# Soft-MoE after a gated recurrence: two output rows of batch 3 from the last weight's chunks, a slot sum in two PSUM banks

## The chip, the cores and the metric

The kernel runs on one core of one Trainium2 chip. Times are device microseconds of one execution, and lower is better. Engines are named as in the profile: PE is the matmul engine, PEld its weight loads, DVE the vector engine, ACT the scalar engine, POOL the GpSimd engine, SP the engine that issues most DMAs. L12 is line 12 of the kernel that the sentence speaks of; where the two kernels' lines differ, it is said which is meant.

## What is computed

The input is `x` and `f_logit` (4 batches, 5056 tokens, 256 channels). A gated recurrence along the tokens is followed by a soft mixture of 8 experts with 4 slots each (32 slots), weights `w1` (8, 256, 1024) and `w2` (8, 1024, 256):

```python
f = lower_bound + (1 - lower_bound) * sigmoid(f_logit)
h[t] = f[t] * h[t-1] + (1 - f[t]) * x[t]
logits = h @ phi                              # (20224, 32)
d = softmax(logits over all tokens)           # one column per slot
slot_input = d.T @ h                          # (32, 256), four slots per expert
slot_out = relu(slot_input @ w1[e]) @ w2[e]   # (32, 256)
out = softmax(logits over the slots) @ slot_out   # (20224, 256)
```

The output, 20.7 MB in float32, can't begin before the last `w2` has been used, since every token mixes all 32 slots.

## The kernel before

The order of the work is written out by hand (`tc.manual_schedule()`), engine by engine in program order. There are three stages.

**The recurrence** (until about 129 us) streams groups of 512 tokens of each batch: load, sigmoid on ACT, product on POOL, transposes on PE, scan on DVE, logits, exponentials into `etall` (partition 32b+s holds slot s of batch b, all tokens along the free side), and the sum `slot_ps`. The 16 weights are loaded from POOL's queue by `load_w` near its end; the last one, `w2_sb[7]`, comes in three parts of four, two and two chunks (a chunk, index `fc`, is 128 of the 1024 hidden units).

**The slot stage** (129 to 143 us) is a chain. `slot_sb` (L597) is turned by four matmuls into `sin_ps` (L601), which lies in the tile `tail`; DVE and ACT make `sin` of it (L611, L612). 32 matmuls (L628) give `hi_ps`, ACT and DVE the two `hi` tiles (L633, L635). They are transposed (L643) and copied: experts 0 to 3 into `hid` (L652), experts 4 to 7 into `wide` by four copies that ACT and DVE take in turn (L659), each of which waits for the one before. `cs_ps` (L645) and `rcs` (L653) are the softmax sum over tokens and its reciprocal. 32 matmuls (L664) sum experts 0 to 3, then a loop over `j` (L674) adds experts 4 to 7, eight matmuls each, into one PSUM tile `so_ps`; for `j == 0` the sum of the first four experts is added by a float32 matmul (L680). Between them stand the `row_sums` matmuls (L391), which sum the exponentials over the slots: 39 rows of 128 tokens, eight of them ahead of L601, eight after `j == 0`, 23 after `j == 1`; DVE's reciprocals (L683, L687, L688) make `rrow` of them. The calls of `spin` (L152) are matmuls whose result nobody reads. DVE writes `slot_out` (L692), POOL a form of it for pairs of batches, `slot_bd` (L694).

**The output stage** multiplies `etall` by `slot_out`. `whole` (L711, then DVE L701 or ACT L705, then the DMA L735) does a block of 16 rows of 128 tokens for one batch; `couple` (L748, then DVE L756 or ACT L753, DMA L765 or L768) does a block for two batches at once. The first block is that of batch 0, and its first DMA takes rows 0 and 1 (row r of a partition's 16 consecutive tokens): 256 KB. All DMAs of this stage stand in SP's queue in program order.

Of the kernel before, what the change touches and what calls it, by code (L numbers as in the profile page):

```python
# [9 lines left out]
F32 = mybir.dt.float32  # L10
BF16 = mybir.dt.bfloat16
# [7 lines left out]
def kernel(  # L19
# [45 lines left out]


    consts = ctx.enter_context(tc.tile_pool(name="consts", bufs=1))
    ident_f = consts.tile([P, P], F32, name="ident_f")
    make_identity(nc, ident_f)
    ident = consts.tile([P, P], BF16, name="ident")  # L70

    rep = consts.tile([P, B, NS], F32, name="rep")

    lb_row = consts.tile([1, D], F32, name="lb_row")
    nc.scalar.dma_start(out=lb_row, in_=lower_bound.unsqueeze(0))
    lbs = consts.tile([P, 2, DC], F32, name="lbs")
    omlb, nomlb = lbs[:, 0], lbs[:, 1]
    phi_f = consts.tile([P, DC, NS], F32, name="phi_f")
    nc.gpsimd.dma_start(out=phi_f, in_=moe_phi.rearrange("(p o) s -> p o s", o=DC))
    phi = consts.tile([P, DC, NS], BF16, name="phi")  # L80

    nc.vector.tensor_copy(ident, ident_f)

    def rep_constants(b):
# [15 lines left out]
    nc.vector.memset(parity, 0.0)  # L100
    for b in range(B):
        nc.vector.memset(parity[ds(b * NS, NS), ds(b % 2, 1)], 1.0)

    def lb_constants():
        row = lb_row.rearrange("u (p o) -> u p o", o=DC)
# [56 lines left out]
    with tc.tile_pool(name="sp2", bufs=3) as sp2, \  # L162
# [437 lines left out]
        for o in range(DC):  # L600
            nc.tensor.matmul(sin_ps[:, o], slot_v[:, o], rep[:, 0],  # L601
                             start=True, stop=True, skip_group_check=True)

    with tc.tile_pool(name="ew", bufs=1) as ew, \
         tc.tile_pool(name="pm", bufs=2, space=PSUM) as pm, \
         tc.tile_pool(name="pbig", bufs=1, space=PSUM) as pbig:

        rep2 = rep.rearrange("p b s -> p (b s)")

        sin = [ew.tile([P, NS], BF16, name=f"sin{o}") for o in range(DC)]  # L610
        nc.vector.tensor_scalar_mul(sin[0], sin_ps[:, 0], omlb[:, ds(0, 1)])  # L611
        nc.scalar.activation(sin[1], sin_ps[:, 1], ACT.Copy, scale=omlb[:, ds(1, 1)])  # L612

        cs1 = ew.tile([P, 1], F32, name="cs1")
        nc.vector.tensor_reduce(cs1, csum, AX.X, ALU.add)


        Q = 4
        H = F // 2
        his = []  # L620
        for q in range(E // Q):
            hi = ew.tile([P, F], BF16, name=f"hi{q}")
            for k in range(2):
# [12 lines left out]
            his.append(hi)  # L636
        cs_ps = pm.tile([P, 1], F32, name="cs_ps", tag="pm")
        rcs = ew.tile([P, 1], F32, name="rcs")
        for q in range(E // Q):
            ht_ps = psu.tile([P, FC, P], BF16, name="ht_ps", tag="up")  # L640
            hi_v = his[q].rearrange("p (c f) -> p f c", f=FC)
            for fc in range(FC):
                nc.tensor.transpose(ht_ps[:, fc], hi_v[:, fc], ident)  # L643
            if q == 0:
                nc.tensor.matmul(cs_ps, rep2, cs1, start=True, stop=True)  # L645
                src = ht_ps.rearrange("p f (j s) -> p f j s", s=NS)[:, :, :, ds(0, SPE)]
                src = bass.AP(tensor=src.tensor, offset=src.offset,
                              ap=[list(src.ap[0]), [P, FC], [NS + SPE, Q], [1, SPE]])
                dst = hid[:, :, :, ds(0, SPE)]
                dst = bass.AP(tensor=dst.tensor, offset=dst.offset,  # L650
                              ap=[list(dst.ap[0]), [Q * NS, FC], [NS + SPE, Q], [1, SPE]])
                nc.scalar.copy(dst, src)  # L652
                nc.vector.reciprocal(rcs, cs_ps)  # L653
                continue
            for j in range(Q):
                s0 = (Q + j) * SPE
                src = ht_ps[:, :, ds(j * NS + s0, SPE)]
                copy = nc.scalar.copy if j % 2 == 0 else nc.vector.tensor_copy
                copy(wide[:, :, j, :, ds(s0, SPE)],  # L659
                     src.unsqueeze(2).broadcast_to([P, FC, B, SPE]))  # L660
        so4_ps = pm.tile([P, D], F32, name="so4_ps", tag="pm")
        for e in range(Q):
            for fc in range(FC):
                nc.tensor.matmul(so4_ps[ds(fc % 4 * NS, NS), :], hid[:, fc, e],  # L664
                                 w2_sb[e][:, fc],
                                 start=(e == 0 and fc < 4),
                                 stop=(e == Q - 1 and fc >= FC - 4),
                                 skip_group_check=True)
        so4 = ew.tile([P, D], F32, name="so4")
        nc.vector.tensor_copy(so4, so4_ps)  # L670
        so_ps = pm.tile([P, D], F32, name="so_ps", tag="pm")
        for j in range(Q):
            for fc in range(FC):
                nc.tensor.matmul(so_ps, wide[:, fc, j].rearrange("p b s -> p (b s)"),  # L674
                                 w2_sb[Q + j][:, fc], start=j == 0 and fc == 0,
                                 stop=j == Q - 1 and fc == FC - 1, skip_group_check=True)
# [12 lines left out]
            if j == 2:  # L689
                spin(tail[:, 0], 6, NS)  # L690
        spin(tail[:, 0], 4, D)
        nc.vector.tensor_scalar_mul(slot_out, so_ps, rcs)  # L692
        for u in range(2):
            nc.gpsimd.tensor_scalar_mul(slot_bd[:, u], slot_out, parity[:, ds(u, 1)])  # L694


    held.close()
    with tc.tile_pool(name="osb", bufs=3) as osb:

        def by_vector(ob, op, scale):  # L700
            nc.vector.tensor_tensor(ob, op, scale.broadcast_to(list(ob.shape)), ALU.mult)  # L701
# [19 lines left out]
        pout = ctx.enter_context(tc.tile_pool(name="pout", bufs=8, space=PSUM))  # L721

        def whole(i, b, pieces, ends):
            n_r = blocks[i][1]
            dst = rows_of(i, b)
            ob = osb.tile([P, n_r, D], F32, name="ob", tag="ob")
            done = 0
            for j, r, k in pieces:
                op = pout.tile([P, 2, D], F32, name="op", tag="op")
                share(op, i, b, r, k)  # L730
                (by_vector, by_scalar)[j](ob[:, ds(r, k)], op[:, ds(0, k)],
                                          scale_of(i, b, r, k))
                if r + k in ends:
                    q = ds(done, r + k - done)
                    nc.sync.dma_start(out=dst[:, q], in_=ob[:, q])  # L735
                    done = r + k
# [35 lines left out]
        def rest():  # L772
# [21 lines left out]
        whole(0, 1, [(t % 2, 2 * t, 2) for t in range(wide_r // 2)], (wide_r,))  # L794
        rest()
        for i in range(end):
            for j in range(B // 2):
                if i or j:
                    couple(i, j)


# [28 lines left out]
```

## Time and profile before

| | us |
|---|---|
| median of the 3 runs (lowest, highest) | 197.96 (197.47, 198.5) |
| the profiled execution's own time | 197.27 |
| its span, first to last instruction | 195.5 |
| PE, DVE, ACT, POOL busy | 152.8, 147.2, 137.3, 103.3 |
| DMA, mean over the span | 362 GB/s |

The page's second part cuts the span into 40 slices of 4.9 us. Its DMA line shows the share of time in which the 16 DMA engines were busy, its PEclk line the clock that was granted to PE, in tenths. PEclk is low in slices 6 and 7 (5 and 8) and in the last ten (5).

### The profile page before, as it was taken

Reading aid. Unit: us, or ns where it says so; the run is one execution under the profiler, and the core shown is the slowest. Engines: PE = TensorE matmul, PEld = TensorE weight load, DVE = VectorE, ACT = ScalarE, POOL = GpSimd, SP = SyncE. Lnnn points to the kernel's source line nnn. Section 1 sums busy time; section 2 is a strip of 40 time slices with the busy share of each in tenths; the row PEclk is TensorE's granted clock in tenths of the full one; section 3 lists DMA queues with packets and bytes.
Section 4 is the critical chain, followed back from the end, with each engine's and each line's share of the span. In section 5 each row is a group of like instructions: output and inputs, shape, how many; then the busy total and the mean of one; then the engine's idle time right before and its main releaser. Section 6 shows DMA issues by size and latency. Waiting matters only on the chain.

```text
span 195.5 us, 3260 instructions
## 1 busy us (share of the span) xinstructions
PE 152.8 (78%) x1205; PEld 105.0 (54%) x1205; DVE 147.2 (75%) x188; ACT 137.3 (70%) x188; POOL 103.3 (53%) x78
## 2 busy tenths in 40 slices
PE   1687589977998979899797887989999999990000
PEld 1465448765685767668586675557974433220000
DVE  2669858999889999999999999814279897771000
ACT  3688674899998998989987597544069987682000
POOL 2589578575999779774969969392030000000000
PEclk9999958999999999999999999999995555555555
DMA  6999999999999999999999999999939999999995
GB/s 206 421 417 424 429 424 429 429 422 393 341 424 431 416 322 427 427 408 347 366 423 413 260 213 214 215 215 213 164 148 420 427 454 419 436 432 429 429 429 221
DMA packets 14145, 70.75 MB, mean 362 GB/s; under 512 B 1569, under 2 KB 2594, under 8 KB 10162
## 3 DMA queue, kind: packets, MB, share of 16 engines
q1 hardware_dynamic: 11504, 62.13, 76.8%
q0 software_dynamic: 2624, 8.42, 21.6%
q8 instruction: 9, 0.15, 0.3%
q14 instruction: 6, 0.05, 0.1%
q10 hardware_dynamic: 2, 0.00, 0.0%
HBM read 58.23 MB, written 20.71 MB: 404 GB/s over the span
## 4 chain that ended last, share of the span: by engine, by line
PE 37%; DVE 26%; ACT 11%; DMA 8%; issue 5%; POOL 2%; SPq 0%; ACTq 0%; DVEq 0%; POOLq 0%
DVE h L313 20%; PE op L748 10%; DMA f_t<-in_f_logit_dram 8%; DVE ht L343 5%; PE hp L326 4%; ACT oc L753 4%; PE sp L261 3%; ACT s_t L235 3%; PE up L267 3%; PE lg L357 2%; POOL u_t L246 2%; PE op L711 2%; PE slot_ps L183 2%; PE so_ps L674 2%; PE slot_ps L408 1%
## 5 line engine op out<-in xcount | busy, mean ns | idle before, releaser
L246 POOL TENSOR_TENSOR u_t<-s_t,x_t 128x1024 bf16<-128x1024 bf16 (+1 forms) x39 | 82.5, 2132 | 23.6 <-ACT s_t L235 10.4
L313 DVE TENSOR_TENSOR_SCAN h<-a,h,up 128x512 bf16<-128x512 f32 (+1 forms) x72 | 87.0, 1252 | 3.5 <-PE up L267 1.8
L235 ACT ACTIVATE s_t<-f_t 128x2048 bf16<-128x2048 f32 (+2 forms) x23 | 38.3, 1668 | 4.0 <-DMA f_t<-in_f_logit_dram 3.7
L326 PE MATMUL hp<-ident_f,h 128*128 128x128 f32 (+1 forms) x160 | 29.4, 308 | 7.9 <-DVE ht L343 6.8
L326 PEld LDWEIGHTS hp<-ident_f,h 128*128 128x128 f32 (+1 forms) x160 | 23.6, 207 | 18.1 <-DVE ht L343 12.4
L748 PE MATMUL op<-slot_bd,etall 64*128 64x512 bf16 x62 | 26.4, 581 | 1.0 <-ACT oc L753 0.3
L295 ACT ACTIVATE a<-sp,lbs 128x1024 f32<-128x1024 bf16 x24 | 25.4, 1112 | 1.3 <-PE sp L261 1.0
L261 PE MATMUL sp<-ident_f,s_t 128*128 128x128 f32 x144 | 21.0, 288 | 6.7 <-ACT s_t L235 4.2
L753 ACT ACTIVATE oc<-op,rrow 128x256 f32<-128x256 f32 x54 | 22.2, 489 | 5.0 <-PE op L748 4.8
L756 DVE TENSOR_TENSOR oc<-op,rrow 128x512 f32<-128x512 f32 x35 | 22.4, 685 | 3.4 <-PE op L748 3.3
L261 PEld LDWEIGHTS sp<-ident_f,s_t 128*128 128x128 f32 x144 | 16.9, 148 | 8.8 <-ACT s_t L235 5.1
L302 ACT ACTIVATE a<-sp,lbs 128x512 f32<-128x512 bf16 (+2 forms) x22 | 17.8, 857 | 3.8 <-PE sp L261 3.5
L267 PE MATMUL up<-ident_f,u_t 64*128 64x64 f32 x192 | 17.6, 229 | 2.1 <-POOL u_t L246 2.1
L183 PE MATMUL slot_ps<-rep,ident_f 128*128 128x256 f32 x54 | 18.2, 432 | 0.6 <-POOL rep L86 0.6
L748 PEld LDWEIGHTS <-etall 64*128 64x128 bf16 x62 | 8.9, 150 | 17.4 <-issue 13.1
L343 ACT COPY ht<-hp 128x512 f32<-128x512 f32 (+1 forms) x18 | 10.5, 583 | 10.2 <-PE hp L326 10.2
L267 PEld LDWEIGHTS up<-ident_f,u_t 64*128 64x128 f32 x192 | 13.9, 138 | 6.0 <-POOL u_t L246 2.5
L343 DVE COPY ht<-hp 128x512 f32<-128x512 f32 (+1 forms) x22 | 14.7, 668 | 2.4 <-PE hp L326 2.4
L705 ACT ACTIVATE ob<-op,rrow 128x256 f32<-128x256 f32 x15 | 6.0, 475 | 7.7 <-PE op L711 7.7
L313 DVE TENSOR_TENSOR_SCAN h<-a,up 128x512 bf16<-128x512 f32 x8 | 9.3, 1208 | 2.5 <-ACT a L302 1.7
L183 PEld LDWEIGHTS slot_ps<-rep,ident_f 128*128 128x128 f32 x54 | 8.8, 199 | 3.0 <-issue 1.1
L261 PE MATMUL up<-ident_f,u_t 128*128 128x128 f32 x48 | 9.5, 329 | 0.7 <-POOL u_t L246 0.6
(110 smaller groups left out, 148.3 us busy)
## 6 DMA issues: line engine op xcount, KB each, us to landing
f_t<-in_f_logit_dram SPq DMA_DIRECT2D x12, 1024.0 KB, 11.7
x_t<-in_x_dram SPq DMA_DIRECT2D x12, 1024.0 KB, 11.1
out_dram<-oc SPq DMA_DIRECT2D x6, 2048.0 KB, 13.1
w_sb<-in_moe_w_dram POOLq DMA_DIRECT2D x14, 512.0 KB, 9.7
f_t<-in_f_logit_dram SPq DMA_DIRECT2D x12, 512.0 KB, 8.5
x_t<-in_x_dram SPq DMA_DIRECT2D x12, 512.0 KB, 8.6
out_dram<-ob SPq DMA_DIRECT2D x1, 2048.0 KB, 10.4
out_dram<-oc SPq DMA_DIRECT2D x2, 896.0 KB, 6.9
```

What stands on the lines that cost most here:

```text
L183: nc.tensor.matmul(slot_bank[:, 1], ident_f, wide_rep, start=False, stop=False, skip_group_check=True)
L235: nc.scalar.activation(s_t, f_t, ACT.Sigmoid, scale=-1.0)
L246: nc.gpsimd.tensor_tensor(uts[n][:, :r], s_t[:, :r], x_t[:, :r], ALU.mult)
L261: nc.tensor.transpose(ps[:, :, r], t[:, r], ident_f)
L267: nc.tensor.transpose(v[:, :, r], t(r)[k].bitcast(F32), ident_f[k, k])
L295: nc.scalar.activation(a, sp[:, :, :, :, o], ACT.Identity, scale=nomlb[:, ds(o, 1)], bias=1.0)
L313: nc.vector.tensor_tensor_scan(h[:, :T, o], decays[n // 2, o][:, n % 2, :T], up[:, :T, o], hs[number(g - 1, b)][:, ds(used(g - 1) - 1, 1), ...
L326: nc.tensor.transpose(hp[:n_p, r], hw[:, :n_p, r], ident_f)
L343: copy(hts[g][:n_p, b].rearrange("p r d -> p (r d)").bitcast(F32), hps.pop(n)[:n_p].rearrange("p r c -> p (r c)"))
L748: nc.tensor.matmul(op.rearrange("p u d -> p (u d)"), ew[:, :, r], slot_bd[ds(j * 2 * NS, 2 * NS)].rearrange("s u d -> s (u d)"), start=Tru ...
L753: nc.scalar.activation(ob[:, u, r], op[:, u], ACT.Copy, scale=scale[:, r, ds(u, 1)])
L756: nc.vector.tensor_tensor(ob[:, :, r], op, scale[:, r].unsqueeze(2).broadcast_to([P, 2, D]), ALU.mult)
```

## The change

All lines here are those of the changed kernel. Four things change.

- **Constants share a tile.** `ident_f`, `ident`, `rep` and `lb_row` become views of one tile `base`; its space is used again for the two rows `begun`. A new column `own` (a reduction on DVE at the start, L104) is 1 on the partitions of the last expert's slots.
- **Two rows of batch 3 directly.** The last expert's hidden values times `own * rcs` are written as `hm` by POOL (L671, 32 partitions by 512 elements, after a product of one column on DVE, L669). Four matmuls (L686) multiply them with the exponentials of two rows, and DVE and ACT copy the two results (128 by 512 each) to `gain` (L688). `add` (L698) then multiplies `gain` by the last four chunks of `w2_sb[7]`, straight into the two rows' PSUM sums. What the other experts and chunks give comes by `slot_pre` (L706, L729). ACT and DVE scale the two rows (L738, L740), and SP sends them as the first output DMA (L742, 256 KB). The block that `whole` does first is batch 3's, from row 2 on, with DMAs of 2, 2, 4 and 6 rows; its second call does batch 2, and the pairs of batches that remain are chosen to match.
- **The slot sum in two banks.** `so_ps` ends after the first four chunks of the last weight and is scaled to `slot_so` (L705); a second tile takes the last four chunks, and `slot_out` is made of both (L732).
- **Order and waits.** 11 row sums move from the loop to just behind the `sin_ps` matmuls (L605), five to before the transposes (L640); 4 stay at `j == 0`, 11 at `j == 1`. Of the spins, the two groups of five and the group of four go, and the group of six becomes eight. The pools of the output stage get `reuse_waits="tile"`: an instruction waits for the earlier users of its own tile's space, not for those of the whole pool's.

In the program as built, PE's order from the last expert sums on is: the 32 matmuls L677; the four L686, the first of which waits for POOL's `hm`; `j == 0`, the float32 matmul (L717, waits for DVE's `so4`, which stands behind the copy to `gain` in DVE's queue), four row sums; `j == 1`, 11 row sums and the left-over rows; `j == 2`, eight spins, which wait for DVE's reciprocals; then `j == 3` as in the diff. DVE's `sin` (L614) waits for the last of the 11 row sums that now follow `sin_ps`, since both are in the tile `tail`; in the kernel before, it waits for the last `sin_ps` matmul. DVE's product L669 stands behind its second copy to `wide` (L663).

```diff
+    own = lbs[:, 2, ds(0, 1)]
+    nc.vector.tensor_reduce(own, ident_f[:, ds(P - SPE, SPE)], AX.X, ALU.add)
...
             nc.tensor.matmul(sin_ps[:, o], slot_v[:, o], rep[:, 0],
                              start=True, stop=True, skip_group_check=True)
+        row_sums(8, 19)
...
             his.append(hi)
+        row_sums(19, 24)
...
+        top = ds((B - 1) * NS, NS)
+        early = etall[top, ds(0, P * wide_r)].rearrange("s (p r) -> s r p", r=wide_r)
+        DIR = 2
+        half = FC // 2
+        nc.vector.tensor_tensor(own, own, rcs, ALU.mult)
+        hm = ew.tile([P, half, P], BF16, name="hm")
+        nc.gpsimd.tensor_scalar_mul(hm[top], his[-1].rearrange("p (c f) -> p f c", f=FC)[
+            top, ds(half, half)], own[top])
+        gain = ew.tile([P, half, DIR, P], BF16, name="gain")
...
+        for i in range(0, half, 2):
+            g_ps = (psu.tile([P, 2, DIR, P], F32, name="g_ps", tag="up") if i == 0 else
+                    pbig.tile([P, 2, DIR, P], F32, name="g_ps", tag="hi_ps0"))
+            for k in range(2):
+                nc.tensor.matmul(g_ps[:, k], hm[top, i + k], early[:, ds(0, DIR)],
+                                 start=True, stop=True, skip_group_check=True)
+            (nc.scalar.copy if i else nc.vector.tensor_copy)(gain[:, ds(i, 2)], g_ps)
...
+        def add(r, fcs, start):
+            for fc in fcs:
+                nc.tensor.matmul(rows_ps[r], gain[:, fc - half, r], w2_sb[E - 1][:, fc],
+                                 start=start and fc == fcs[0], stop=fc == FC - 1,
+                                 skip_group_check=True)
+
         for j in range(Q):
             for fc in range(FC):
+                if j == Q - 1 and fc == half:
+                    nc.vector.tensor_scalar_mul(slot_so, so_ps, rcs)
+                    nc.vector.tensor_copy(slot_pre[top], slot_so[top])
+                    so_ps = pm.tile([P, D], F32, name="so_ps", tag="pm")
...
-                if j == Q - 1 and fc in (FC // 2 - 1, FC // 4 * 3 - 1):
-                    spin(tail[:, 0], 5, NS)
+                if j == Q - 1 and fc == half + 1:
+                    for r in range(DIR):
+                        add(r, (half, half + 1), True)
...
-                row_sums(8, wide_r)
+                row_sums(24, 28)
...
-                row_sums(wide_r, n_grp * R)
+                row_sums(28, n_grp * R)
...
-                spin(tail[:, 0], 6, NS)
-        spin(tail[:, 0], 4, D)
-        nc.vector.tensor_scalar_mul(slot_out, so_ps, rcs)
+                spin(tail[:, 0], 8, NS)
+        for r in range(DIR):
+            nc.tensor.matmul(rows_ps[r], early[:, r], slot_pre[top],
+                             start=False, stop=False, skip_group_check=True)
+            add(r, (FC - 2, FC - 1), False)
+        nc.vector.scalar_tensor_tensor(slot_out, so_ps, rcs, slot_so, ALU.mult, ALU.add)
...
+        for r in range(DIR):
+            scale = rrow[:, r, ds(B - 1, 1)]
+            if r == 0:
+                nc.scalar.activation(begun[:, r], rows_ps[r], ACT.Copy, scale=scale)
+            else:
+                nc.vector.tensor_tensor(begun[:, r], rows_ps[r], scale.broadcast_to([P, D]),
+                                        ALU.mult)
+        nc.sync.dma_start(
+            out=out[ds((B - 1) * S, P * wide_r)].rearrange(
+                "(p r) d -> p r d", r=wide_r)[:, ds(0, DIR)], in_=begun)
...
-    with tc.tile_pool(name="osb", bufs=3) as osb:
+    with tc.tile_pool(name="osb", bufs=3, reuse_waits="tile") as osb:
...
-        whole(0, 0, ((0, 0, 1), (1, 1, 1), (0, 2, 2), (1, 4, 2), (0, 6, 2), (1, 8, 2),
-                     (0, 10, 2), (1, 12, 2), (0, 14, 2)), (2, 4, 8, 12, 16))
+        whole(0, B - 1, ((0, 2, 1), (1, 3, 1), (0, 4, 2), (1, 6, 2), (0, 8, 2),
+                         (1, 10, 2), (0, 12, 2), (1, 14, 2)), (4, 6, 10, 16))
```

More of the change, by code (lines that the diff above doesn't have):

```diff
@@ L67 @@
     consts = ctx.enter_context(tc.tile_pool(name="consts", bufs=1))
-    ident_f = consts.tile([P, P], F32, name="ident_f")
+    phi_f = consts.tile([P, DC, NS], F32, name="phi_f")
+    phi = consts.tile([P, DC, NS], BF16, name="phi")
+    base = consts.tile([P, 2 * P + P // 2 + D], F32, name="base")
+    ident_f = base[:, ds(0, P)]
     make_identity(nc, ident_f)
-    ident = consts.tile([P, P], BF16, name="ident")
-    rep = consts.tile([P, B, NS], F32, name="rep")
-    lb_row = consts.tile([1, D], F32, name="lb_row")
+    ident = base[:, ds(P, P // 2)].bitcast(BF16)
+    rep = base[:, ds(P + P // 2, P)].rearrange("p (b s) -> p b s", b=B)
+    lb_row = base[ds(0, 1), ds(2 * P + P // 2, D)]
+    begun = base[:, ds(0, 2 * D)].rearrange("p (r d) -> p r d", r=2)
     nc.scalar.dma_start(out=lb_row, in_=lower_bound.unsqueeze(0))
-    lbs = consts.tile([P, 2, DC], F32, name="lbs")
+    lbs = consts.tile([P, 4, DC], F32, name="lbs")
     omlb, nomlb = lbs[:, 0], lbs[:, 1]
-    phi_f = consts.tile([P, DC, NS], F32, name="phi_f")
+    own = lbs[:, 2, ds(0, 1)]
     nc.gpsimd.dma_start(out=phi_f, in_=moe_phi.rearrange("(p o) s -> p o s", o=DC))
-    phi = consts.tile([P, DC, NS], BF16, name="phi")
     nc.vector.tensor_copy(ident, ident_f)
@@ L671 @@
         so_ps = pm.tile([P, D], F32, name="so_ps", tag="pm")
+        slot_so = ew.tile([P, D], F32, name="slot_so")
+        slot_pre = ew.tile([P, D], BF16, name="slot_pre")
+        rows_ps = [tail[:, 0, ds(0, D)], psu.tile([P, 2, D], F32, name="row_ps", tag="up")[:, 0]]
+        def add(r, fcs, start):
[3 more added lines that the diff above has]
+                                 skip_group_check=True)
         for j in range(Q):
             for fc in range(FC):
+                if j == Q - 1 and fc == half:
+                    nc.vector.tensor_scalar_mul(slot_so, so_ps, rcs)
+                    nc.vector.tensor_copy(slot_pre[top], slot_so[top])
+                    so_ps = pm.tile([P, D], F32, name="so_ps", tag="pm")
                 nc.tensor.matmul(so_ps, wide[:, fc, j].rearrange("p b s -> p (b s)"),
-                                 w2_sb[Q + j][:, fc], start=j == 0 and fc == 0,
-                                 stop=j == Q - 1 and fc == FC - 1, skip_group_check=True)
-                if j == Q - 1 and fc in (FC // 2 - 1, FC // 4 * 3 - 1):
-                    spin(tail[:, 0], 5, NS)
+                                 w2_sb[Q + j][:, fc],
+                                 start=(j, fc) in ((0, 0), (Q - 1, half)),
+                                 stop=j == Q - 1 and fc in (half - 1, FC - 1),
+                                 skip_group_check=True)
+                if j == Q - 1 and fc == half + 1:
+                    for r in range(DIR):
+                        add(r, (half, half + 1), True)
             if j == 0:
@@ L719, in rows_of @@
             return out[ds(b * S + t0, P * n_r)].rearrange("(p r) d -> p r d", r=n_r)
-        pout = ctx.enter_context(tc.tile_pool(name="pout", bufs=8, space=PSUM))
+        pout = ctx.enter_context(tc.tile_pool(name="pout", bufs=8, space=PSUM, reuse_waits="tile"))
         def whole(i, b, pieces, ends):
@@ L726, in whole @@
             ob = osb.tile([P, n_r, D], F32, name="ob", tag="ob")
-            done = 0
+            done = pieces[0][1]
             for j, r, k in pieces:
@@ L789 @@
         end = len(blocks) - 1
-        whole(0, 0, ((0, 0, 1), (1, 1, 1), (0, 2, 2), (1, 4, 2), (0, 6, 2), (1, 8, 2),
-                     (0, 10, 2), (1, 12, 2), (0, 14, 2)), (2, 4, 8, 12, 16))
+        whole(0, B - 1, ((0, 2, 1), (1, 3, 1), (0, 4, 2), (1, 6, 2), (0, 8, 2),
+                         (1, 10, 2), (0, 12, 2), (1, 14, 2)), (4, 6, 10, 16))
         couple(end, 0, (4, 7))
         couple(end, 1)
-        whole(0, 1, [(t % 2, 2 * t, 2) for t in range(wide_r // 2)], (wide_r,))
+        whole(0, B - 2, [(t % 2, 2 * t, 2) for t in range(wide_r // 2)], (wide_r,))
         rest()
@@ L797 @@
             for j in range(B // 2):
-                if i or j:
+                if i or j < B // 2 - 1:
                     couple(i, j)
```

## The prediction

> **What bounds the kernel now.** I read the slices first, then the busy times by stage, then the slot stage instruction by instruction. The page's slices:
>
> ```profile
> PEclk9999958999999999999999999999995555555555
> DMA  6999999999999999999999999999939999999995
> GB/s 206 421 417 424 429 424 429 429 422 393 341 424 431 416 322 427 427 408 347 366 423 413 260 213 214 215 215 213 164 148 420 427 454 419 436 432 429 429 429 221
> ```
>
> From slice 31 on the DMA engines are full to the end: the output stage runs at the rate of its writes. Slice 30 is the only one with a hole. The windows around it (us, busy time of five engines, PE clock, DMA share, GB/s):
>
> ```profile
> 140.00:141.00 1.00, 1.00 (x13) 0.79 (x11) 0.76 (x2) 0.00 (x0) 0.00 (x0) 1.00 0.78 128
> 141.00:142.00 1.00, 1.00 (x22) 0.93 (x21) 0.00 (x0) 0.00 (x0) 0.00 (x0) 1.00 0.23 37
> 144.00:145.00 1.00, 0.98 (x9) 0.83 (x8) 1.00 (x3) 1.00 (x4) 0.97 (x2) 1.00 0.08 25
> 145.00:146.00 1.00, 0.97 (x5) 0.65 (x6) 1.00 (x3) 1.00 (x4) 0.00 (x0) 1.00 1.05 404
> ```
>
> The weights are in by 142, the first output moves just before 145, then the writes never stop until 193.4. So the end is the issue of the first output DMA plus a constant, and I price the change by that one instant. The timeline of the chain up to it (start, length):
>
> ```profile
> 135.91 0.22 DVE L659 COPY wide<-ht_ps 128x128 bf16<-128x128 bf16 x1 [0.33 <-ACT wide L659]
> ...
> 142.06 0.38 PE L674 MATMUL so_ps<-w_t,wide 128*128 128x256 bf16 x2
> ...
> 142.47 0.48 DVE L692 TENSOR_SCALAR slot_out<-so_ps,rcs 128x256 bf16<-128x256 f32 x1 [1.54 <-PE so_ps L674]
> ...
> 144.09 3.10 SPq L735 DMA_DIRECT2D out_dram<-ob  x5
> ```
>
> The last weight part is issued at 127.5 and lands 14.6 us later (the shortest of the four in the view of tile `w_t`), at 142.06: the last two L674 start on it. PE is no less tight: of 135.80 to 142.06 its windows show no idle time, and only the 16 short spins (0.025 us each) are free there. From 142.06 to the issue at 144.09 it takes 2.03 us.
>
> **The change, step by step.** Lines of the changed kernel; times on the clock of this profile.
>
> *Row sums moved forward.* 23 of them took 1.54 us at 138.59, so 0.06 each. DVE's `sin` now waits for 11 of them: 0.66 later. Five more stand before the transposes, 0.3, of which about 0.2 falls where PE waited for `hi` (L628's last start to L643). I take 0.7 for the whole chain from `sin` on, so the last copy to `wide` ends at 136.13 + 0.7 = 136.83, and PE is done with the 32 matmuls of L677 at 135.85 + 0.7 = 136.55. In total PE does no more row sums than before.
>
> *`hm` on POOL.* Behind that copy DVE multiplies a column (0.15, as L653 and L688: 0.17 and 0.11): 136.97. POOL starts 0.19 after its releaser (142.95 to 143.14 at L694): 137.15. The product itself isn't in the trace. Its neighbours:
>
> ```profile
> L694 POOL TENSOR_SCALAR slot_bd<-slot_out,parity 128x256 bf16<-128x256 bf16 x2 | 1.8, 923 | 9.6 <-DVE slot_out L692 9.6
> L115 POOL TENSOR_SCALAR phi<-phi_f,lbs 128x32 bf16<-128x32 f32 x2 | 1.5, 777 | 3.6 <-DMA phi_f<-in_moe_phi_dram 3.6
> L86 POOL COPY rep<-ident_f 32x128 f32<-32x128 f32 x4 | 1.1, 285 | 0.2
> L401 POOL COPY left<-etall 32x64 bf16<-32x64 bf16 x4 | 1.0, 258 | 0.1
> ```
>
> L694 is the same operation with the same factor column: 0.92 for 256 elements. L115's shorter instance takes 0.357 for 32. The line through both gives 512 elements 1.57. Lower end, by the copies on 32 partitions (0.258 for 64, 0.285 for 128): 0.45. Upper end, twice L694: 1.85. I take 1.57, from the nearest row. PE can start L686 at 137.15 + 1.57 + 0.06 = **138.78**, having stood since 136.55: a stall of 2.2 us. Behind L686 in PE's queue is everything that makes `slot_out`.
>
> [...]
>
> *From L686 on PE* (+ counts from its first start): four matmuls of 256 columns, 0.11 each as in L674, +0.44. `j == 0`, eight, +1.31. DVE copies the first pair to `gain` (+0.46, 0.69 as L635) and only then `so4` (0.41, as L670), ready at +1.48, so L717 waits until +1.54. L717 0.44, four row sums 0.25, eight matmuls 0.87, 11 row sums and the left-over 0.72, eight matmuls 0.87: +4.69. The spins wait for the reciprocals (left-over start to spin start was 139.97 to 140.99, so 1.02): +4.78, then 0.2. Four chunks 0.43, two 0.22, four `add` 0.44: the last two chunks start at +6.07, which is 144.85. They landed at 142.06: the wait for the weights is gone, PE is late in its place. `slot_so` (0.48, as L692) and `slot_pre` (0.3, from L82's 0.226 for 128 elements) end at +6.42; the six row matmuls then run to +7.30. DVE makes `slot_out` meanwhile (0.5), then scales row 1 (+7.33, 0.425 as the first L701); SP issues at +7.82 = **146.60**, against 144.09: 2.51 later.
>
> *Edits at no cost.* The reduction at the start (0.15) falls into the 2.6 us in which DVE waits for the first load at L242. Shared constants add no wait in the built order. Tile-wise waits: L701 started 0.42 after L711, a matmul takes 0.27 of it, so at most 0.1 is to be had; I count nothing. SP gets one more DMA ahead of the pairs of batches; its issues are 0.6 apart (five in 3.10), as long as 256 KB take at 404 GB/s, so it keeps up, and the pairs are ready some 4.0 us after the first issue as before (148.13), with 2 MB (4.9 us) in front of them. Bytes and the last DMA are unchanged.
>
> **Sum.** 197.27 + 2.51 = 199.78 on the profiled execution. That one lies 0.69 under the median of 197.96, so 200.5 as a median. With POOL at its ends: 199.4 and 200.8.
>
> **The rivals.**
>
> 1. *PE's clock halves after the stall.* The trace has one idle time of PE as long, and what came of it (timeline, start and length; then the windows, with the clock third from the end):
>
> ```profile
> 23.21 1.09 PE L261 MATMUL sp<-ident_f,s_t 128*128 128x128 f32 x8 [1.96 <-ACT s_t L235]
> ```
>
> ```profile
> 21.00:24.40 3.40, 1.44 (x14) 1.25 (x13) 3.05 (x3) 2.22 (x3) 1.21 (x2) 0.99 1.04 435
> 24.40:27.80 3.40, 2.75 (x16) 1.10 (x13) 2.45 (x2) 3.40 (x3) 3.26 (x3) 0.50 1.01 422
> 27.80:31.20 3.40, 3.40 (x17) 2.95 (x14) 1.84 (x2) 0.46 (x1) 1.87 (x2) 0.50 1.00 424
> 31.20:34.60 3.40, 3.40 (x31) 3.18 (x29) 3.07 (x4) 2.79 (x4) 2.62 (x2) 1.00 1.01 429
> ```
>
> 1.96 us idle, and the clock was half for the next 6.8 us. 16 L711 took 1.97 us at the full clock and 3.63 at half, so a half clock over the 5 us of PE work behind the stall costs up to 3.5, over 3.4 us of it 1.6; I take 2.0: median 202.5. Against it: that window was busy for 1.44 us of 3.4, ours for about 1.6 if it falls alike, and idle times near 1 us changed nothing. [...]
>
> 2. *POOL is quick.* At the copies' rate the stall is 1.1 us: 197.27 + 1.39 = 198.66, median 199.4.
>
> 3. *The change does what it says: faster.* If L686 starts by 135.9, the last chunks are met at 142.06, the six row matmuls end at 143.09, DVE at 143.55, SP issues at 143.62: 0.47 earlier, median 197.5. The point that decides is that start, and PE itself is free only at 136.55; it would need the weights to land some 2.8 us later than here, so that PE's lateness hides.
>
> 4. *Nothing measurable*: the two offset each other, 197.0 to 198.9.
>
> **How the numbers follow.** Forecast 200.5: 0.45. Clock halved, 202.5: 0.26. POOL quick, 199.4: 0.14. Faster, 197.5: 0.08. Within 0.5% (about what a measurement of this kernel tells from no change): 0.07. So slower 0.85, same 0.07, faster 0.08. The range runs from 198.6 to 202.8: it leaves out the faster case, most of "same", and the dearest part of the halved clock, together under 2 in 10. The forecast's own range is 199.6 to 201.0.
>
> **What would show it.** In the profile after: PE L686 waits for POOL's `hm` L671 by 1 us or more; `hm` takes near 1.6; `sin` L614 starts about 0.7 later; the last pair of L708 starts near 144.9, long after the landing; L742 is issued near 146.6; the hole in the DMA grows from 3 to over 5 us. PEclk at 5 between 140 and 147 is rival 1. Wrong if L686 never waits, or if L742 is issued before 144.1.

## The result, and the profile after

The changed kernel takes 203.75 us in the median of 6 runs, the kernel before 197.6 us in the median of 6 beside it; the ratio is 1.0286, with a 95% interval of 1.0249 to 1.0324. Slower was forecast, by 2.5 us; it is some 6. The comparisons leave disturbed executions out, and of one kernel (e11) the profile was of such a one and is not read.

The profiled execution of the changed kernel took 202.42 us, with a span of 200.7 us against 195.5. Its page, the slices of 5.0 us:

```profile
PEclk9999889999999999999999999999797555555555
DMA  5999999999999999999999999999119999999994
```

The hole in the DMA has grown from one slice to two (29 and 30, at 1 tenth). PEclk reads 7 in slice 29 (140.5 to 145.5), where the kernel before read 9. The windows of the changed kernel (columns as in the prediction: stretch, length, five engines' busy time, PE clock, DMA share, GB/s):

```profile
136.00:138.50 2.50, 0.01 (x2) 0.00 (x0) 0.24 (x2) 0.00 (x0) 2.05 (x1) 1.00 1.06 209
139.68:143.08 3.40, 3.40 (x13) 1.86 (x12) 0.98 (x2) 0.59 (x1) 0.00 (x0) 0.50 0.44 73
143.10:146.50 3.40, 3.40 (x46) 3.06 (x45) 1.31 (x3) 0.00 (x0) 0.00 (x0) 1.00 0.00 0
149.00:150.00 1.00, 1.00 (x12) 1.00 (x11) 1.00 (x4) 0.92 (x3) 1.00 (x2) 1.00 0.02 8
150.00:151.00 1.00, 1.00 (x8) 0.57 (x7) 1.00 (x3) 1.00 (x4) 0.00 (x0) 1.00 0.97 375
```

In the first almost nothing but POOL works; in the second PE is busy throughout, at half the clock, with 13 matmuls where the third, equally long, holds 46 (some of these are the shorter row sums). No output leaves until 149. The timeline of the chain (start, length; in brackets the idle time before and its releaser):

```profile
136.42 2.05 POOL L671 TENSOR_SCALAR hm<-hi,lbs 32x512 bf16<-32x512 bf16 x1 [2.83 <-DVE lbs L669]
138.52 1.99 PE L686 MATMUL g_ps<-etall,hm 32*128 32x256 bf16 x4 [2.52 <-POOL hm L671]
140.45 1.89 PE L708 MATMUL so_ps<-w_sb,wide 128*128 128x256 bf16 x8
142.13 1.06 PE L717 MATMUL so_ps<-so,base 128*128 128x256 f32 x2
143.28 1.04 PE L708 MATMUL so_ps<-w_sb,wide 128*128 128x256 bf16 x8
...
147.09 0.38 PE L708 MATMUL so_ps<-w_t,wide 128*128 128x256 bf16 x2
...
147.50 0.26 PE L729 MATMUL tail<-slot_pre,etall 32*128 32x256 bf16 x1
...
147.70 0.39 PE L698 MATMUL tail<-w_t,gain 128*128 128x256 bf16 x2
...
148.02 0.33 PE L729 MATMUL row_ps<-slot_pre,etall 32*128 32x256 bf16 x1
...
148.28 0.39 PE L698 MATMUL row_ps<-w_t,gain 128*128 128x256 bf16 x2
...
148.71 0.42 DVE L740 TENSOR_TENSOR base<-row_ps,rrow 128x256 f32<-128x256 f32 x1 [0.71 <-PE row_ps L698]
...
149.20 0.35 SPq L742 DMA_DIRECT2D out_dram<-base  x1
149.66 0.87 SPq L785 DMA_DIRECT2D out_dram<-ob  x2
```

The recurrence ended 0.76 earlier in this execution (DVE's copy to `slot_sb` starts at 129.03, before at 129.79), so I count from that copy. From it to the issue of the first output DMA it took 14.30 before and takes **20.17** now: 5.87 more, where 2.51 was forecast. From the issue to the span's end it is 51.41 before and 51.50 now. So 5.87 − 0.76 + 0.09 = 5.2, the difference of the spans: all but 0.1 of it lies ahead of that issue. (The medians are 6.15 apart. The instant at which the recurrence ends differs between executions, from 128.9 to 130.8 in the profiled ones below, so the distance from the copy is the steadier measure.)

### The profile page after: what moved, and what is told of

Its sections match the earlier page's. It is cut to its first block, busy times and chain, and to the rows that moved or that the text cites. A ratio compares the mean times of both kernels' runs of the same rounds, so it can differ in the third digit from the quotient of the medians.

```text
span 200.7 us, 3270 instructions
## 1 busy us (share of the span) xinstructions
PE 156.2 (78%) x1205; PEld 106.7 (53%) x1205; DVE 148.4 (74%) x193; ACT 138.0 (69%) x190; POOL 105.3 (52%) x79
## 4 chain that ended last, share of the span: by engine, by line
PE 35%; DVE 23%; DMA 14%; ACT 9%; POOL 5%; issue 4%; ACTq 0%; SPq 0%; DVEq 0%; POOLq 0%
DVE h L315 17%; DMA x_t<-in_x_dram 14%; PE op L798 9%; DVE ht L345 4%; POOL u_t L248 4%; ACT oc L803 4%; PE hp L328 3%; PE up L269 3%; PE so_ps L708 2%; PE sp L263 2%; PE op L761 2%; PE lg L359 2%; PE slot_ps L185 1%; PE tail L393 1%; PE slot_ps L410 1%
## 5 line engine op out<-in xcount | busy, mean ns | idle before, releaser
L328 PE MATMUL hp<-base,h 128*128 128x128 f32 (+1 forms) x160 | 29.3, 307 | 8.1 <-DVE ht L345 6.9
L328 PEld LDWEIGHTS hp<-base,h 128*128 128x128 f32 (+1 forms) x160 | 23.3, 207 | 18.2 <-DVE ht L345 12.8
L263 PE MATMUL sp<-base,s_t 128*128 128x128 f32 x144 | 21.9, 296 | 6.0 <-ACT s_t L237 4.1
L263 PEld LDWEIGHTS sp<-base,s_t 128*128 128x128 f32 x144 | 17.6, 152 | 7.9 <-ACT s_t L237 5.0
L269 PE MATMUL up<-base,u_t 64*128 64x64 f32 x192 | 17.9, 230 | 2.2 <-POOL u_t L248 2.2
L185 PE MATMUL slot_ps<-base 128*128 128x256 f32 x54 | 17.7, 423 | 0.0
L269 PEld LDWEIGHTS up<-base,u_t 64*128 64x128 f32 x192 | 14.0, 138 | 6.2 <-POOL u_t L248 2.6
L263 PE MATMUL up<-base,u_t 128*128 128x128 f32 x48 | 9.7, 335 | 0.6 <-POOL u_t L248 0.6
L185 PEld LDWEIGHTS slot_ps<-base 128*128 128x128 f32 x54 | 8.6, 193 | 2.3 <-issue 1.1
L359 PE MATMUL lg<-h,phi 128*32 128x512 bf16 (+1 forms) x80 | 9.6, 389 | 0.0
```

The costliest lines, as they stand in the source:

```text
L185: nc.tensor.matmul(slot_bank[:, 1], ident_f, wide_rep, start=False, stop=False, skip_group_check=True)
L263: nc.tensor.transpose(ps[:, :, r], t[:, r], ident_f)
L269: nc.tensor.transpose(v[:, :, r], t(r)[k].bitcast(F32), ident_f[k, k])
L328: nc.tensor.transpose(hp[:n_p, r], hw[:, :n_p, r], ident_f)
```

## The experiments

Two theories were stated for the excess of 3.4 us over the forecast, and a rival for each. **The clock theory:** the stall before L686 halves PE's clock, at a price of 1.0 to 1.25; the rival is that the matmuls are slow for another reason. **The step theory:** each L686 takes 0.45 because its moving operand `early` steps through SBUF by 32 bytes (16 elements of two bytes); the rivals are the half clock and the 32 partitions. In the table "distance" is from the start of the `slot_sb` copy to the issue of the first output DMA, "issue" is that instant in the profiled execution. Each ratio is to runs of the kernel before on the same chip, whose medians were 197.4 to 197.9 in the experiments.

| kernel | median us (runs) | ratio to before, 95% interval | distance | issue |
|---|---|---|---|---|
| before | 197.6 (6) | | 14.30 | 144.09 |
| after | 203.75 (6) | 1.0286 [1.0249, 1.0324] | 20.17 | 149.20 |
| e1 spins in the stall | 201.99 (4) | 1.0228 [1.0181, 1.0276] | 18.92 | 148.40 |
| e2 flat operand | 203.03 (4) | 1.0254 [1.0208, 1.0301] | 19.16 | 149.92 |
| e3 `hm` on DVE | 202.2 (4) | 1.0234 [1.0204, 1.0264] | 18.86 | 149.47 |
| e4 block late | 199.04 (10) | 1.0077 [1.0046, 1.0108] | 16.29 | 146.25 |
| e5 late and flat | 198.2 (10) | 1.0031 [1.0008, 1.0055] | 15.31 | 145.79 |
| e6 and `sin_ps` apart | 197.88 (10) | 1.0006 [0.9986, 1.0027] | 15.42 | 144.33 |
| e7 `slot_pre` matmuls first | 197.5 (12) | 0.9992 [0.9971, 1.0014] | 14.93 | 144.04 |
| e9 before, row sums moved | 197.34 (10) | 0.9991 [0.9972, 1.0010] | 14.80 | 144.18 |
| e10 before, waits by tile | 197.72 (10) | 0.9997 [0.9977, 1.0018] | 14.14 | 144.98 |
| e11 pair first | 197.51 (12) | 0.9985 [0.9964, 1.0006] | | |
| e12 the kernel of e11 | 197.52 (12) | 1.0001 [0.9982, 1.0021] | 15.07 | 143.97 |

The intervals of e1 to e3 touch that of after; what is said of them rests on the traces, one execution each. e8, a kernel with extra work, isn't in the table.

### e1: the stall filled

Eleven matmuls that nobody reads keep PE busy while POOL makes `hm`.

```diff
+        spin(tail[:, 0], 11, H)
         for i in range(0, half, 2):
```

> The changed kernel with 11 unread matmuls of 512 columns (some 2.4 us at the full clock) put ahead of the four L686, into the time in which PE waits for hm; hm and L686 start no earlier. Measure: D, from the start of the slot_sb copy to the issue of the first output DMA; 14.30 us in the kernel before, 20.17 in the changed one. Theory 1 (PE standing still for 2.5 us halves its clock, which cost 1.0 here): the clock stays full until the first output DMA, j == 0 to its row sums take 1.8 instead of 2.8, D near 19.1, time about 1 us under the changed kernel's. Rival (the clock halves there for another reason, such as the low use of the array by L686 itself): it halves all the same, D stays near 20.2.

The page and the timeline of e1:

```profile
PEclk9999799996999999999999999999999555555555
```

```profile
136.87 2.06 POOL L671 TENSOR_SCALAR hm<-hi,lbs 32x512 bf16<-32x512 bf16 x1 [3.32 <-DVE lbs L669]
138.99 2.00 PE L687 MATMUL g_ps<-etall,hm 32*128 32x256 bf16 x4
140.91 1.05 PE L709 MATMUL so_ps<-w_sb,wide 128*128 128x256 bf16 x8
```

In the slot stage the clock stays full, the eight matmuls of `j == 0` take 1.05 in place of 1.89, and the distance falls by 1.25. The clock theory holds here, and e4 to e7 and e12, which have no such stall, have the full clock there too (1.00 in their windows from 144 to 145); e3 and e8 show that idle time isn't the whole of it. The four matmuls take as long as in after, 138.99 to 140.91, at the full clock throughout: the half clock isn't what makes them slow.

### e2: a flat operand

ACT copies the two rows side by side ahead of time, and the four matmuls read the copy.

```diff
+        flat = ew.tile([P, DIR, P], BF16, name="flat")
+        nc.scalar.copy(flat[top], early[:, ds(0, DIR)])
...
-                nc.tensor.matmul(g_ps[:, k], hm[top, i + k], early[:, ds(0, DIR)],
+                nc.tensor.matmul(g_ps[:, k], hm[top, i + k], flat[top],
```

> The changed kernel, but ACT first copies the exponentials of the two rows side by side, and the four L686 read that copy instead of etall, in which neighbouring elements of a row are 32 bytes apart. Theory 2 (the step of the moving operand makes L686 slow): L686 starts come 0.11 us apart instead of 0.46, D falls by about 1.4, to 18.8. Rival (the 32-partition form or the half clock makes them slow): the spacing stays over 0.2 and D near 20.2.

```profile
138.15 2.04 POOL L671 TENSOR_SCALAR hm<-hi,lbs 32x512 bf16<-32x512 bf16 x1 [4.69 <-DVE lbs L669]
140.25 0.60 PE L688 MATMUL g_ps<-flat,hm 32*128 32x256 bf16 x4 [2.52 <-POOL hm L671]
```

The same four matmuls on the same 32 partitions now start 0.11 apart, and the group takes 0.60 in place of 1.99. The step theory holds. The distance fell by 1.01 and not by 1.4: the clock still halves (the float32 matmul of `j == 0` takes 1.06, as in after, where e1 has 0.60), and now more of the matmuls behind the block lie in that stretch (from `j == 1` to the last two chunks it takes 4.32 in place of 3.81).

### e3: `hm` on DVE

```diff
-        nc.gpsimd.tensor_scalar_mul(hm[top], his[-1]
+        nc.vector.tensor_scalar_mul(hm[top], his[-1]
```

> The changed kernel with hm written by DVE instead of POOL. Theory (POOL's 2.05 us for hm is most of PE's stall): hm takes 0.3 to 0.6 on DVE, PE's stall falls from 2.5 to about 0.9, idle times of that length didn't halve the clock elsewhere, so D falls by 1.6 and a further 1.0, to about 17.6. Rival (L686 alone brings the half clock): D about 18.6, with a half clock after L686.

```profile
137.86 0.67 DVE L671 TENSOR_SCALAR hm<-hi,lbs 32x512 bf16<-32x512 bf16 x1
138.59 2.00 PE L686 MATMUL g_ps<-etall,hm 32*128 32x256 bf16 x4 [1.00 <-DVE hm L671]
140.52 1.89 PE L708 MATMUL so_ps<-w_sb,wide 128*128 128x256 bf16 x8
```

The product takes 0.67 in place of 2.05 and the stall shrinks from 2.52 to 1.00. Of these 1.52, 1.31 shows in the distance, since 3.07 us of the half clock lie behind the start of L708 and 2.63 in after. For the clock halved all the same, for 3.41 us (140.18 to 143.59): L708 takes 1.89. I had expected that a stall of 1 us leaves the clock alone, as such idle times did in the recurrence of the kernel before (0.90 to 1.16 us each, with the clock at 1.00 from 31.2 to 147.2); the rival in the expectation was right that it would halve. A stall of 1.0 followed by 1.9 us of the four slow matmuls was enough in this execution.

The recurrence, where the kernels do the same work, shows that an idle time of this length doesn't settle the clock by itself. PE stands for 1.02 us up to 45.82 in e1 and for 1.03 up to 45.86 in after. The windows around and behind it, in e1 and then in after:

```profile
42.94:46.35 3.41, 2.10 (x28) 1.77 (x32) 2.91 (x4) 3.39 (x5) 2.79 (x3) 1.00 1.02 425
46.35:49.76 3.41, 3.41 (x26) 2.67 (x19) 3.41 (x4) 3.40 (x3) 1.21 (x1) 0.50 1.05 324
```

```profile
42.94:46.35 3.41, 2.06 (x24) 1.74 (x28) 2.90 (x4) 3.39 (x5) 2.83 (x3) 1.00 1.00 418
46.35:49.76 3.41, 3.15 (x34) 2.18 (x30) 3.41 (x4) 3.40 (x3) 1.18 (x1) 1.00 1.04 318
```

PE is busy about as little in the first window, and the clock behind it is half in one execution and full in the other. In the traces of before and after the clock changes only at instants that lie multiples of 3.41 us apart (24.36, 31.18 and 147.23 in before; 23.62, 27.03, 139.67, 143.08 and 153.32 in after), and where an idle time falls between them differs between executions: counted on from 27.03, the instants around the 1.03 us of after are about 44.1 and 47.5, while in e1 the clock changed at 46.35. That may be the reason; it isn't shown. So the halved clock of e3 is what one execution had, and another may not have it.

### e4, e5, e6: the block moved, then made flat, then `sin` freed

e4 moves the four matmuls with their copies behind the row sums of `j == 1`, where `hm` has long been ready. e5 adds the flat operand of e2. e6 adds a PSUM tile of its own for `sin_ps`, so that `sin` no longer waits for the row sums.

```diff
-        for i in range(0, half, 2):
-            g_ps = ...
...
             if j == 1:
                 row_sums(28, n_grp * R)
+                for i in range(0, half, 2):
+                    g_ps = ...
```

```diff
-        sin_ps = tail[:, 0, ds(G // 2, DC * NS)].rearrange("p (o s) -> p o s", o=DC)
+        sin_ps = psu.tile([P, G], F32, name="sin_ps", tag="up")[
+            :, ds(0, DC * NS)].rearrange("p (o s) -> p o s", o=DC)
...
-        row_sums(8, 19)
+        row_sums(8, 17)
```

(The later groups of row sums in e6 are 17 to 20 and 21 to 27.)

> The changed kernel with the four L686 and the copies to gain moved in PE's order to behind the last row sums of j == 1, by when hm is long there. Theory (the stall and the half clock behind it are 3.5 of the 5.9 that D grew): no stall, full clock, L686 still 1.9 long, D about 16.6, time about 3.5 us under the changed kernel's and 2.3 over the kernel before. Rival (PE's order doesn't matter, the later DVE copies or something else bind): D over 18.

> The changed kernel with both earlier edits: the four L686 behind the row sums of j == 1, and reading the side by side copy. Theory (stall, half clock and strided operand are separate terms): D = 16.29 - 1.4 = 14.9, so 0.6 over the kernel before, which is the late sin (0.7). Rival (L686 was hidden behind something once it was late): D stays near 16.3.

> As the one with late and side by side L686, and sin_ps in a PSUM tile of its own, so that sin no longer waits for the row sums behind it; 9 row sums stand there and 4 behind the hi matmuls, the rest at j == 0 and j == 1. Theory (sin's wait for the row sums is the 0.7): sin starts 1.25 after slot_sb as before, D falls by up to 0.7, to 14.2 to 14.4, where the landing of the last chunks (12.2 after slot_sb in the kernel before) holds the last two so_ps matmuls. The design as drawn then gains next to nothing over 14.30. Rival (the direct rows save 0.5 once nothing is late): D 13.8.

e4 took 3.88 off the distance: no stall, the full clock (1.00 from 144 to 147, and 1.05 for the eight matmuls behind the block), and the block alone still costs its 1.9. e5 took off another 0.98, not the 1.4 that was expected: the spins behind `j == 2` wait for DVE's reciprocals, which stand behind the copy to `gain`, so from the start of `j == 2` to the spins it now takes 1.29 in place of 0.88. In e6 `sin` starts 1.25 behind `slot_sb` again, not 1.95, yet the distance didn't fall, and that expectation missed. The timeline of e6:

```profile
142.26 0.38 PE L704 MATMUL so_ps<-w_t,wide 128*128 128x256 bf16 x2
142.57 0.33 PE L732 MATMUL tail<-slot_pre,etall 32*128 32x256 bf16 x1
...
144.32 1.25 PE L764 MATMUL op<-slot_out,etall 32*128 32x256 bf16 x10 [0.51 <-DVE base L743]
144.33 0.35 SPq L745 DMA_DIRECT2D out_dram<-base  x1
...
145.23 0.34 SPq L788 DMA_DIRECT2D out_dram<-ob  x1
```

PE is early enough again and the landings bind. The third part of the weight lands at 141.55 and PE starts on it at 141.59; with the four products of `add` between, it comes to the last pair at 142.26, 0.08 after the landing of the last part at 142.18. The landings don't move with `slot_sb` (the last one is at 142.0 to 142.2 in the profiled executions of before, after and e6). From here the instant of the issue is the measure, not the distance. And here the design can be read nearly as it was drawn: with PE 0.08 late, the first output DMA leaves 2.07 after the last pair, where the kernel before needed 2.03.

### e7, e11, e12: a shorter tail

e7 puts the two `slot_pre` matmuls ahead of the last pair and drops the eight spins. e11 puts them behind the pair but ahead of all four products of `add`, so that weights of 32 and 128 rows change places twice and not four times; e12 is the same kernel again. The edit of e11 against e6, without the spins:

```diff
         for r in range(DIR):
             nc.tensor.matmul(rows_ps[r], early[:, r], slot_pre[top],
                              start=False, stop=False, skip_group_check=True)
+        for r in range(DIR):
             add(r, (FC - 2, FC - 1), False)
```

> As the one before it, and the two matmuls of slot_pre stand ahead of the last two so_ps matmuls, so that only four matmuls of 128 rows follow the last chunks, and the eight spins go. Theory (after the last chunks the order of 32-row and 128-row matmuls costs 0.2 at each change, and slot_pre is late): from the last two so_ps to the first output DMA 1.4 instead of 2.1, D 13.6 to 13.8 if PE is there in time, time 0.3 to 0.6 us under the kernel before. Rival (PE is late by itself): the last two start over 12.5 after slot_sb, D 14.0 or more, the time the same as before.

> The run with the slot_pre matmuls moved ahead of the last pair, with these two matmuls put behind the last pair again, still in front of all four products of the last chunks. If the wait for slot_pre, which held the last pair to 142.69 although its chunks had landed at 142.14, is what took the gain back, the pair starts within 0.15 of the landing (142.3), slot_pre (ready 142.3) costs its matmuls nothing, one change of weights between 32 and 128 rows is left in place of three, and the first output DMA is issued 1.55 to 1.75 behind the pair, at 143.85 to 144.0 where before had 144.09; the ratio is 0.998 to 1.0. If the design had more to give, the issue would be at or under 143.6 and the ratio under 0.998. If the wait moves into the tail (slot_pre later than the pair's end by over 0.2), the issue stays at 144.1 or later.

> The kernel of e11 once more, for its profile: that of e11 was of a disturbed execution of 206.53 us, while its other eleven runs lie between 197.36 and 197.95. Expected as there: the last pair within 0.15 of the landing of its chunks, the first output DMA issued 1.55 to 1.75 behind the pair, at 143.85 to 144.0; the ratio 0.9985 again, within 0.002. The rival: slot_pre comes later than the pair's end by over 0.2, and the issue stays at 144.1 or later.

In e7 the issue comes 1.35 behind the pair, as expected, but the pair itself starts at 142.69, though its chunks landed at 142.14. The expectation of e11 puts this down to the wait for `slot_pre`; the trace shows little of such a wait. `slot_pre` is ready at 142.30, and the weight load of the first of its matmuls, behind a gap of 0.21, starts at 142.32, the matmul at 142.35. What holds the pair is mainly the two matmuls themselves with a change of weights on either side. So PE was late, which is the rival of e7's expectation. In e12 the pair starts at 142.15. Its timeline:

```profile
142.15 0.38 PE L704 MATMUL so_ps<-w_t,wide 128*128 128x256 bf16 x2
...
142.47 0.33 PE L730 MATMUL tail<-slot_pre,etall 32*128 32x256 bf16 x1
...
142.57 0.48 DVE L734 SCALAR_TENSOR_TENSOR slot_out<-so_ps,rcs,slot_so 128x256 bf16<-128x256 f32 x1 [0.34 <-PE so_ps L704]
...
143.96 1.68 PE L763 MATMUL op<-slot_out,etall 32*128 32x256 bf16 x14 [0.52 <-DVE base L742]
...
143.97 0.35 SPq L744 DMA_DIRECT2D out_dram<-base  x1
...
144.87 0.82 SPq L787 DMA_DIRECT2D out_dram<-ob  x2
```

The issue is at 143.97, 1.82 behind the pair (1.55 to 1.75 expected) and 0.12 earlier than before. The time is the same nonetheless. The second output DMA is issued 0.90 behind the first, against 0.41 before, and 256 KB move in about 0.62 (at 420 GB/s, the rate of 146 to 147 in before), so by this estimate the engines run dry for some 0.3: from the first issue to the span's end it is 51.73 here, 51.41 before. The other kernels bear this out: 51.4 to 51.5 in after and e1 to e5, whose second DMA follows some 0.46 behind the first, 51.7 to 51.8 in e6 and e7, where it follows 0.9 behind. The second DMA needs `slot_out` and PE's L763, and in e6, e7 and e12 L763 waits for DVE to read the directly made row; in e5, without the tile of its own for `sin_ps`, it doesn't. A kernel that has both wasn't tried; by these rows an estimate is 143.97 and 144.43, some 0.1 ahead of before's 144.09 and 144.50.

### e8: the two sizes by themselves

The kernel before with work that nobody reads, in one execution: in place of six spins, groups of four matmuls of 256 columns whose moving operand steps by 1, 2, 4, 8 and 16 elements of `etall`, on 128 and on 32 partitions; ahead of the slot sums, three products on POOL.

```diff
+        nc.gpsimd.tensor_scalar_mul(t_a[top], wide_in[top], parity[top, ds(0, 1)])
+        nc.gpsimd.tensor_scalar_mul(t_b[top], flat_in[top], parity[top, ds(0, 1)])
+        nc.gpsimd.tensor_scalar_mul(t_c, flat_in, parity[:, ds(0, 1)])
...
+                        mv = etall[q, ds(0, D * st)].rearrange("s (p r) -> s r p", r=st)[:, 0]
+                        for _ in range(4):
+                            nc.tensor.matmul(pr, his[-1][q, ds(0, P)], mv,
+                                             start=True, stop=True, skip_group_check=True)
```

> The kernel before, with unread work added for its lengths alone. On PE, in place of the six spins: four matmuls each of 256 columns with steps of 1, 2, 4, 8 and 16 elements in the moving operand, first on 128 partitions, then on 32. On POOL, three products by a factor column: 32 partitions by 512 with a step of 8 elements (as hm), 32 by 512 side by side, 128 by 512 side by side. Theory: the matmuls come 0.11 apart with small steps and over 0.4 at a step of 16, alike for 128 and 32 partitions; POOL takes 2.05 with the step and 1.6 without. Rival: the 32-partition form is slow by itself (over 0.2 at a step of 1); POOL takes 2.05 in all three.

POOL's products and, of PE, two of the weight loads among the matmuls with a step of 8 elements on 128 partitions:

```profile
135.66 2.11 POOL L667 TENSOR_SCALAR t_a<-hi,parity 32x512 bf16<-32x512 bf16 x1 [2.29 <-DVE hi L635]
137.84 1.57 POOL L668 TENSOR_SCALAR t_b<-hi,parity 32x512 bf16<-32x512 bf16 x1
139.50 1.57 POOL L669 TENSOR_SCALAR t_c<-hi,parity 128x512 bf16<-128x512 bf16 x1
...
144.45 0.12 PEld L705 LDWEIGHTS <-hi 128*128 128x128 bf16 x1 [0.33 <-issue]
144.90 0.12 PEld L705 LDWEIGHTS <-hi 128*128 128x128 bf16 x1 [0.34 <-issue]
```

The loads come 0.45 apart, as the four matmuls of the block do. The starts of the matmuls by step, in us from one to the next:

| step, elements of 2 bytes | 1 | 2 | 4 | 8 | 16 |
|---|---|---|---|---|---|
| 128 partitions, full clock | 0.11 | 0.11 | 0.22 | 0.45 | 0.46 |
| 32 partitions, half clock from 147.94 on | 0.21 | 0.21 | 0.23 | 0.45 | 0.46 |

From 8 elements on the two rows agree (0.45 and 0.46): neither the half clock nor the 32 partitions add anything. On POOL the input's step of 16 bytes costs 0.54, and 32 partitions take as long as 128.

The half clock in the table has no idle time ahead of it. The windows on either side of its start:

```profile
144.53:147.94 3.41, 3.41 (x10) 0.79 (x9) 0.00 (x0) 0.00 (x0) 0.00 (x0) 1.00 0.00 0
147.94:151.35 3.41, 3.41 (x15) 1.75 (x14) 0.00 (x0) 0.00 (x0) 0.00 (x0) 0.50 0.00 0
```

In the first, PE is busy throughout by the profile, all but its last 0.2 us with matmuls at steps of 16 and 32 bytes, and the clock halves behind it. So the half clock came behind some 3 us of slow matmuls without a stall; behind the 1.9 us of them in e1 and e4 it did not come. In e3 the 3.41 us ahead of the half clock (136.77 to 140.18) hold 1.0 us of idle time and 1.6 us of such matmuls. How much of each it takes no run tells.

### e9 and e10: two parts of the change on the kernel before

e9 moves the row sums, as the change does; e10 sets `reuse_waits="tile"` on the two output pools.

```diff
+        row_sums(8, 19)
...
+        row_sums(19, 24)
...
-                row_sums(8, wide_r)
+                row_sums(24, 28)
```

```diff
-    with tc.tile_pool(name="osb", bufs=3) as osb:
+    with tc.tile_pool(name="osb", bufs=3, reuse_waits="tile") as osb:
```

(The pool `pout` is changed in the same way.)

> The kernel before with the moves of the row sums alone: 11 behind the matmuls of sin_ps, five ahead of the transposes, four at j == 0, 11 at j == 1. Both theories: sin starts 0.7 later behind slot_sb (1.95 in place of 1.25), since it lies in the tile that the row sums write, and the matmuls of the hidden values shift by 0.7 to 0.8. Theory 1 (the moved sums are on the path that sets the end): the first output DMA is issued 0.3 to 0.8 later than 144.1, so the ratio is 1.0015 to 1.004. Rival (they only take time from PE's wait for the last part of the last weight, which lands at 142.0 to 142.2 in every run so far): the issue stays at 144.1 within 0.2 and the ratio is 1 within 0.002. 16 of the sums were behind the first expert products before and no longer are, which pays back some 0.9 of PE by the last chunks, so I hold the rival for likelier here.

> The kernel before with the waits of the two output pools tile by tile alone. The expectation of the prediction, nothing: the first output DMA is issued at 144.1 and the span ends 51.4 behind it, 0.1 either way; ratio 1 within 0.002. The rival, that pool-wide waits held the output back: the distance of the issue from the end of the span falls by more than 0.2.

The timeline of e9:

```profile
130.36 0.86 PE L391 MATMUL tail<-ones,etall 128*128 128x128 bf16 x11
131.33 0.25 DVE L612 TENSOR_SCALAR sin<-tail,lbs 128x32 bf16<-128x32 f32 x1 [1.53 <-PE tail L391]
...
142.16 0.38 PE L676 MATMUL so_ps<-w_t,wide 128*128 128x256 bf16 x2
...
144.18 0.82 SPq L737 DMA_DIRECT2D out_dram<-ob  x2
```

`sin` starts 1.95 behind `slot_sb`, 0.7 later, and the last pair still meets the landing: fewer row sums stand in PE's way afterwards. The rival held, the move costs nothing by itself. e10 changes nothing that can be measured either. Its issue is at 144.98 and not at 144.1, because the copy to `slot_sb` starts 1.05 later in that execution; it comes 1.87 behind the pair, against 2.03, and 51.5 ahead of the span's end, against 51.4, which its time doesn't show.

## Why the prediction was wrong, point by point

The sign and the path were right: PE waits for `hm` on POOL (2.52 us), everything that makes `slot_out` stands behind the wait, and the last chunks are met long after their landing, at 147.09. The size was not: 200.5, range 198.6 to 202.8, against 203.75. The terms, on the distance of 20.17:

| step of the prediction | forecast | measured | difference |
|---|---|---|---|
| row sums ahead of `sin`, to the last copy to `wide` | +0.70 | +0.81 | +0.11 |
| from there to the start of `hm` | 0.32 | 0.24 | −0.08 |
| `hm` on POOL | 1.57 | 2.05 | +0.48 |
| four L686, to the first matmul of `j == 0` | 0.44 | 1.93 | **+1.49** |
| `j == 0` with its float32 matmul and row sums | 1.79 | 2.83 | **+1.04** |
| `j == 1` to the last two chunks | 3.84 | 3.81 | −0.03 |
| last two chunks to the issue | 1.75 | 2.11 | +0.36 |

The differences add up to 3.37, the excess of 3.36 within rounding. Without the 1.49 of L686 they would have led to 202.4, inside the range; without the 1.04 of `j == 0`, to 202.8, at its upper end.

- **"Four matmuls of 256 columns, 0.11 each as in L674, +0.44"** is the step that failed. L674's moving operand lies side by side, that of L686 steps by 32 bytes; the two are the same shape and not the same row. e2 and e8 settle it: 0.11 with the flat copy, 0.46 with the step. In e8 it is 0.11 at steps of 2 and 4 bytes, 0.22 at 8, 0.45 at 16 and 0.46 at 32.
- **`hm` at 1.57** was the right price for an input that lies side by side: e8 measured 1.57. The input here is `hi` read with a step of 16 bytes, which makes it 2.04 to 2.11, above even the upper end that I gave (1.85). In e8 the step costs a third more for the whole instruction, 2.11 against 1.57.
- **The halved clock** was priced as the second case (0.26) and came true, for 3.41 us. Its cost was 1.26, by e1, where `j == 0` with what follows takes 1.57 at the full clock and not 2.83 (the forecast's 1.79 had 0.22 to spare, so the table has 1.04); I had taken 2.0. I weighed the idle time against the idle time of the recurrence in one trace and left out that the four slow matmuls would follow it. (At the rates that stand beside it, 1.97 against 3.63, the 3.5 given for 5 us of work would be 4.2.) No run had shown the 3.4 us for which the price of 1.6 was given: the half clock in the recurrence of before lasted 6.82 us (24.36 to 31.18); after and e3 then showed 3.41 in the slot stage. What starts it isn't shown: it came behind 1.96 us of idle time in before, behind 2.52 in after and behind none in e8.
- **The tail at 1.75** left out that weights of 32 rows and of 128 rows take turns on PE four times. At each turn the profile shows a gap of 0.12 to 0.21 ahead of the weight load, put down to issue. The six row matmuls take 1.17 from the first one's start to the last one's end, where the sum had 0.88: 0.29 of the 0.36.
- **The faster rival, 0.47 earlier if PE comes in time,** was mispriced too: it has the issue 1.56 behind the last pair. In all kernels with the tail as changed (after, e1 to e5) the first output DMA follows the last pair by 2.1 and the second by 2.6, and in e6, where PE is all but in time, the first by 2.07; before it was 2.03 and 2.44. The direct rows save the wait for `slot_out`, but six matmuls and their turns take its place, and the second DMA needs `slot_out` anyway.
- Right as forecast: `sin` 0.7 later, the hole in the DMA of over 5 us, no gain from the waits by tile that a time shows, the constant behind the first issue.

Repaired step by step (e4 to e7, e11, e12), the change comes back to the time of the kernel before, and not measurably below it: 0.9985 to 1.0006 in e6, e7, e11 and e12, with 1 in each interval. That it can't go below isn't shown, since the kernel with both the early pair and the early second DMA wasn't tried.

## What to carry to other kernels

Take a matmul's duration from a row with the same operands: its shape and also the step at which the moving operand is read; 32 bytes made it four times as long (0.46 in place of 0.11), and a copy made off the path takes that away (0.11 in e2). Before moving the first output forward, work out when the second can follow; a first DMA that left 0.12 early gained nothing here, as the next came 0.3 later than the first one took. A stall of PE can be paid twice, here with 2.52 as idle time and 1.26 in the matmuls at half clock behind it.

## What the runs showed of the hardware that was not expected

- PE, 256 columns: 0.11 us at steps of 2 and 4 bytes, 0.22 at 8, 0.45 at 16, 0.46 at 32, and from 16 bytes on the same at half clock and on 32 partitions (e8).
- POOL, 512 elements with a factor column: 1.57 on 32 and on 128 partitions, 2.11 when the input steps by 16 bytes; DVE does the latter in 0.67 (e8, e3).
- The clock halved for 3.41 us after only 1.00 us of idle PE, with four matmuls at a step of 32 bytes behind it (e3); with the same four matmuls and no idle time ahead it stayed full (e1, e4).
- It halved with no idle time at all behind some 3.2 us of matmuls at steps of 16 and 32 bytes, with PE busy by the profile (e8).
- The same idle time of 1.02 to 1.03 us in the recurrence was followed by a half clock in one execution (e1) and by the full clock in another (after).
